# Reciprocals of the gate's real part on VectorE in place of exponentials on ScalarE

## The chip, the cores and the metric

The kernel runs on one core of one Trainium2 chip. The metric is the device time of one execution in microseconds (us). Before the change the median of three runs is 189.34 us (189.3 to 189.58). Four compute engines work side by side, each with its own instruction stream: TensorE (PE in the profile, PEld for its weight loads), VectorE (DVE), ScalarE (ACT) and GpSimd (POOL). SyncE (SP) issues most of the loads and stores. An engine works through its own stream in order and waits at an instruction until what that instruction needs is done.

## The reference

A gated linear attention with complex gates is followed by a normalised two-layer network with a residual. Per batch and head there is a running complex state of 48 x 48 that decays and turns by the gate at every one of 768 time steps:

```python
mag = np.sqrt(a_re * a_re + a_im * a_im)
scale = np.minimum(mag, 0.999) / (mag + 1e-06)
a_re_n, a_im_n = (a_re * scale, a_im * scale)
for t in range(S):
    new_re = ar * S_re - ai * S_im
    new_im = ar * S_im + ai * S_re
    S_re, S_im = (new_re + kv, new_im)        # kv: outer product of k and v at t
    y[:, :, t] = np.einsum('bhd,bhde->bhe', q[:, :, t], S_re)
```

Then, on x, the heads of y side by side (4 x 768 x 384): `x + relu(norm(x) @ w_ch1) @ w_ch2`, with 384 and 1536 columns. All tensors are float32; a_re lies between 0.85 and 0.95.

## The kernel before, in words

**Tiling.** The 768 steps of each of the 4 batches are cut into 6 chunks of 128 steps, and two chunks make a pair. There are 12 pairs, P = 0 to 11, three to a batch. One pair's gates are a tile of 128 partitions by 768 elements (8 heads x 2 steps x 48 columns). Pair 0 is worked in two halves of 4 heads, so its gate operations have 384 elements and come twice (names 0.0 and 0.1); those of pair 1 have 768 (name 1.0).

**From gate to decay and angle.** With a_re and a_im loaded into the tiles `are` and `aim`, the steps of one pair (or half) X are, in order of need:

- ln.X (line 452, ScalarE): w = ln(are)
- iv.X (line 454, ScalarE): are = exp(-w), that is 1/are, written over the tile that ln.X has read
- r.X: r = aim * are, the ratio of imaginary to real part (VectorE or GpSimd, helper line 293)
- r2.X (line 462 where ScalarE does it, else helper line 293): r2 = r * r
- u.X (line 466, ScalarE): r2 = ln(1 + r2)
- l.X and lc.X (lines 470 and 473, VectorE): l = w + r2 / 2, the log of the gate's magnitude, and its cap
- dec.X (line 481, TensorE): sums of l over time; en.X and e.X (line 485, ScalarE) are exponentials of it
- th.X (line 489, ScalarE) is the arctangent of r, ph.X (lines 506 to 514, TensorE) its sums over time, and sine and cosine follow from those

From them come the scaled keys and queries (ke, qe, ks, qs), the products over a chunk (am, atm), the state (G), the output y and x, and then the two-layer network (mm1, relu, mm2, ot, st).

**What sets the order.** One table, PLAN, written out by hand, holds every step with the letter of the engine that does it: A is ScalarE, V VectorE, G GpSimd, S SyncE, P TensorE with its bank. The table's order is the order in each engine's stream. A name behind @ makes a GpSimd step wait for a VectorE step. Waits on data follow from what each step reads and writes.

**Buffers.** `are` has three tiles, used in turn: the load are.3.0 refills the tile of pair 0, and has to wait until r.0.0 and r.0.1 have read it. `w` has two. SyncE issues its loads in order, so a load that waits holds back those behind it.

**TensorE at the start.** The steps named warm (line 805) are matrix products whose results nobody reads; 32 of them stand ahead of dec.0.0 and 22 between dec.0.0 and dec.0.1.

u_th (line 327, VectorE) is a constant that the first ph needs.

Of the kernel before, what the change touches and what calls it, by code (L numbers as in the profile page):

```python
# [13 lines left out]
AF = mybir.ActivationFunctionType  # L14
# [22 lines left out]


PLAN = """
aim.0.0:A are.0.0:S pickf:V tab.log.0:A ln.0.0:A iv.0.0:A are.1.0:S gln:S ue:G cmean:G uth:V r.0.0:V are.0.1:S one:G  # L40
r2.0.0:A u.0.0:A l.0.0:V ln.1.0:A aim.0.1:S ln.0.1:A q.0.1:S iv.0.1:A pick:G@r.0.0 lc.0.0:V warm.0:P0 warm.1:P0
warm.2:P0 warm.3:P0 warm.4:P0 warm.5:P0 warm.6:P0 warm.7:P0 warm.8:P0 warm.9:P0 warm.10:P0 warm.11:P0 warm.12:P0
warm.13:P0 warm.14:P0 warm.15:P0 warm.16:P0 warm.17:P0 warm.18:P0 warm.19:P0 warm.20:P0 warm.21:P0 warm.22:P0
warm.23:P0 warm.24:P0 warm.25:P0 warm.26:P0 warm.27:P0 warm.28:P0 warm.29:P0 warm.30:P0 warm.31:P0 dec.0.0:P6
aim.1.0:S iv.1.0:A r.0.1:V r.1.0:V ident:G pad.e.0:G@r.0.1 are.2.0:S pad.e.1:G zdec:G@r.0.1 r2.1.0:V r2.0.1:A u.0.1:A
l.0.1:V u.1.0:A lc.0.1:V ln.2.0:A l.1.0:V lc.1.0:V q.0.0:S warm.32:P0 warm.33:P0 warm.34:P0 warm.35:P0 warm.36:P0
warm.37:P0 warm.38:P0 warm.39:P0 warm.40:P0 warm.41:P0 warm.42:P0 warm.43:P0 warm.44:P0 warm.45:P0 warm.46:P0
warm.47:P0 warm.48:P0 warm.49:P0 warm.50:P0 warm.51:P0 warm.52:P0 warm.53:P0 dec.0.1:P2 aim.2.0:S en.0.0:A6 pad.qs.2:G
# [103 lines left out]
class Graph:  # L152
# [5 lines left out]
    def add(self, name, emit, needs=(), uses=(), ps=None):  # L158
        assert name not in self.ops, name
        self.ops[name] = Op(name, emit, list(needs), list(uses), ps)  # L160
# [51 lines left out]
def kernel(  # L212
# [12 lines left out]
    nc = tc.nc  # L225
    B, H, S, D = q.shape
# [40 lines left out]
    def T(name, i):  # L267
        return tiles[name][i % RINGS[name]]

    g = Graph(RINGS)  # L270
    act = nc.scalar.activation

    def eng(name):
        return g.ops[name].eng

    def bank(owner, parts=C):
        return banks[0:parts, g.bank[owner]]

    def bank2(owner, parts=C):
        i = g.bank[owner]  # L280
        return banks[0:parts, i:i + 2]
# [16 lines left out]
    def flat(t):  # L298
        return t.rearrange("p h d -> p (h d)")


    ident = pool.tile([C, C], BF16, name="ident")
    u_th = pool.tile([C, R, R, C], FP16, name="u_th")
    u_e = pool.tile([C, R, R, C], FP16, name="u_e")
    pick = pool.tile([C, C], FP16, name="pick")
# [4 lines left out]
    cmean = pool.tile([C, C], FP32, name="cmean")  # L310
    gc = pool.tile([C, ND, C], BF16, name="gc")
    gln = pool.tile([C, ND], FP32, name="gln")
# [54 lines left out]
    for i in range(NG):  # L367
        g.add(f"wl.{i}", lambda i=i: nc.gpsimd.dma_start(
            out=w1b[:, :, ts(i, 512)], in_=moe_w_ch1.rearrange("(dc p) j -> p dc j", p=C)[:, :, ts(i, 512)]))
        g.add(f"wl.{NG + i}", lambda i=i: nc.gpsimd.dma_start(  # L370
            out=w2b[:, ts(i, JG)], in_=moe_w_ch2.rearrange("(jc p) e -> p jc e", p=C)[:, ts(i, JG)]))
# [11 lines left out]
    for jb in range(NG):  # L383
# [7 lines left out]
        for ec in range(ND):  # L391
            g.add(f"wc.{jb}.{ec}", lambda jb=jb, ec=ec, o=o: nc.vector.scalar_tensor_tensor(
                out=w1b[:, ec, ts(jb, 512)], in0=w1b[:, ec, ts(jb, 512)], scalar=gln[:, ds(ec, 1)],
# [3 lines left out]
    def pair_ops(P):  # L397
# [6 lines left out]
        add = g.add  # L404

        for c in range(R):
            for nm, ap in (("k", k), ("q", q), ("vf", v)):
                add(f"{nm}.{P}.{c}", lambda nm=nm, ap=ap, c=c: ring(f"{nm}.{P}.{c}").dma_start(  # L408
                    out=T(nm, P)[:, c],
                    in_=ap[b].rearrange("h (c p) d -> p c h d", p=C)[:, pp * R + c]),  # L410
# [13 lines left out]
        for i in range(NS):  # L424
            hs = ts(i, HS)
            fs = ts(i, W)
            X = f"{P}.{i}"

            def S_(name, n=P, hs=hs):
                return flat(T(name, n)[:, hs])  # L430

            def view(owner):
                if NS == 1:
                    return bank2(owner)[:, :, 0:W]
                return bank(owner)[:, 0:R * W].rearrange("p (c x) -> p c x", c=R)

            def v16(owner=f"ph.{X}", view=view):
                if NS == 1:
                    return bank2(owner).bitcast(I16).rearrange(
                        "p s (x two) -> p s x two", two=2)[:, :, 0:W, 0]  # L440
                return bank(owner).bitcast(I16)[:, 0:2 * R * W].rearrange(
                    "p (c x two) -> p c x two", c=R, two=2)[:, :, :, 0]
# [5 lines left out]
            for nm, ap in (("are", a_re), ("aim", a_im)):  # L448
                add(f"{nm}.{X}", lambda nm=nm, ap=ap, hs=hs, X=X: ring(f"{nm}.{X}").dma_start(
                    out=T(nm, P)[:, hs], in_=ap[b][hs].rearrange(  # L450
                        "h (k p j) d -> p k h (j d)", p=C, j=R)[:, pp]), uses=[(nm, P)])
            add(f"ln.{X}", lambda S_=S_: act(out=S_("w"), in_=S_("are"), func=AF.Ln),
                needs=[f"are.{X}"], uses=[("are", P), ("w", P)])
            add(f"iv.{X}", lambda S_=S_: act(out=S_("are"), in_=S_("w"), func=AF.Exp, scale=-1.0),  # L454
                needs=[f"ln.{X}"], uses=[("are", P), ("w", P)])
            add(f"r.{X}", lambda S_=S_, X=X: tt(f"r.{X}", out=S_("r"), in0=S_("aim"), in1=S_("are"),
                                                op=ALU.mult),
# [11 lines left out]
            def f_l(S_=S_):  # L469
# [4 lines left out]
                out=S_("l"), in0=S_("l"), scalar1=LNCAP, scalar2=LNEPS, op0=ALU.min, op1=ALU.add),  # L474
# [9 lines left out]
            for nm, sc in (("en", -1.0), ("e", 1.0)):  # L484
                add(f"{nm}.{X}", lambda nm=nm, sc=sc, X=X, fs=fs, view=view: act(  # L485
                    out=T(nm, P)[:, 0:R, fs], in_=view(f"dec.{X}"), func=AF.Exp, scale=sc),
# [34 lines left out]
            if not last:  # L521
# [11 lines left out]
                out=T("trig", P)[:, 1, :, fs], in_=v16(), func=AF.Sin, scale=TWO_PI_SAFE / TURN),  # L533
                needs=[f"ph.{X}"], uses=[("trig", P)], ps=(f"ph.{X}", nb))
            if P in QUARTER:
                def f_qt(X=X, view=view):
# [7 lines left out]
                    out=T("trig", P)[:, 0, :, fs], in_=v16(), func=AF.Sin, scale=TWO_PI_SAFE / TURN),  # L544
                    needs=[f"qt.{X}"], uses=[("trig", P)], ps=(f"ph.{X}", nb))
            else:
                def f_abs(X=X, fs=fs, v16=v16):
# [8 lines left out]
                    out=T("trig", P)[:, 0, :, fs], in_=T("sh", P)[:, :, fs], func=AF.Sin,  # L556
                    scale=-TWO_PI_SAFE / TURN, bias=PI / 2),
# [47 lines left out]
        for c in range(R):  # L605
# [26 lines left out]
            def f_am(n):  # L632
# [7 lines left out]
                out=T("atm", n), in_=bank2(f"am.{n}").rearrange("p s (h t) -> p (s h) t", t=C)),  # L640
# [122 lines left out]
        for c in range(R):  # L763
            n = P * R + c
            cuts = [(f".{x}", ts(x, DM // 2)) for x in range(2)] if n == NP * R - 1 else [("", ds(0, DM))]
            for tag, es in cuts:
                own = f"o.{n}{tag}"
                w = DM // len(cuts)
                for part in range(NG):
# [9 lines left out]
                    out=T("ot", n)[:, es], in_=bank(own)[:, 0:w], mul=T("rstd", P)[:, ds(c, 1)]),  # L779
# [3 lines left out]
                def f_ot(n=n, c=c, own=own, es=es, w=w, tag=tag):  # L783
# [12 lines left out]
                    out=out[b].rearrange("(c p) e -> p c e", p=C)[:, pp * R + c, es],  # L796
                    in_=T("ot", n)[:, es]),
                    needs=[f"ot.{n}{tag}"], uses=[("ot", n)])

    for P in range(NP):  # L800
        pair_ops(P)
# [40 lines left out]
```

## Time and profile before

| what | before |
|---|---|
| median of three runs | 189.34 us |
| span of the profiled execution | 187.1 us |
| TensorE busy | 176.4 us, 94% |
| ScalarE busy | 160.0 us, 86% |
| VectorE busy | 153.7 us, 82% |
| GpSimd busy | 111.1 us, 59% |
| iv on 384 elements (ScalarE, 2) | 523 ns each |
| iv on 768 elements (ScalarE, 11) | 844 ns each |

The span reaches from the first to the last instruction of the profiled execution; its full time isn't listed apart, and the runs' median is 2.24 us above the span. A row of the timeline reads: start in us from the span's start, length in us, engine, line, operation, what it writes and reads with shapes and types, how many instructions are merged, and in brackets how long the engine had been idle and what ended that. A tile shown as r may be r2, since the trace leaves numbers out. Tiles of before and after can be told apart by line.

### The profile page before, as it was taken

How to read it: one execution, taken by the hardware profiler on the slowest of the kernel's cores; microseconds unless marked ns; L12 is line 12 of the kernel's file. 1: busy time of each engine (PE TensorE's matmuls, PEld its weight loads, DVE VectorE, ACT ScalarE, POOL GpSimd, SP SyncE). 2: the span in 40 equal slices, each digit the busy share in tenths (PEclk: the TensorE clock that was granted, in tenths of full speed). 3: DMA queues.
4: the chain of work that ended last, by engine and by line, in shares of the span. 5: the costliest groups of instructions: out<-in, count | busy, mean ns of one | idle time of the engine just before them, and what ended most of it. 6: DMA issues, size and time to landing. Idle time of an engine off the chain costs nothing.

```text
span 187.1 us, 5110 instructions
## 1 busy us (share of the span) xinstructions
PE 176.4 (94%) x2025; PEld 135.1 (72%) x2027; DVE 153.7 (82%) x275; ACT 160.0 (86%) x228; POOL 111.1 (59%) x130
## 2 busy tenths in 40 slices
PE   5978898999999999999999999999999998999993
PEld 3756565787767789866687696878867866778772
DVE  1479999999989999999979989899879888866332
ACT  3889999999999989999999999998999897274560
POOL 3328699589207996288176692365879759420600
PEclk9999999999999999999999999999999999999999
DMA  5999999999999999699999997999999969996122
GB/s 148 291 256 227 223 260 189 207 206 194 233 261 239 219 221 191 128 203 309 204 155 238 256 265 92 185 247 169 216 175 215 203 144 229 210 199 173 40 90 84
DMA packets 132439, 37.39 MB, mean 200 GB/s; under 512 B 126528, under 2 KB 132416, under 8 KB 132416
## 3 DMA queue, kind: packets, MB, share of 16 engines
q1 hardware_dynamic: 123040, 32.45, 83.9%
q0 software_dynamic: 2784, 2.36, 8.2%
q10 hardware_dynamic: 6592, 2.26, 4.7%
q8 instruction: 16, 0.26, 0.6%
q14 instruction: 7, 0.06, 0.1%
HBM read 28.31 MB, written 4.72 MB: 177 GB/s over the span
## 4 chain that ended last, share of the span: by engine, by line
PE 71%; DVE 10%; DMA 6%; ACT 4%; POOL 3%; SPq 2%; issue 2%; DVEq 0%; POOLq 0%
PE banks L772 25%; PE banks L740 21%; PE banks L635 5%; PE banks L612 4%; PE banks L506 4%; PE banks L481 4%; DMA aim<-in_a_im_dram 3%; PE banks L685 2%; DMA qsT<-qs 2%; PE banks L706 2%; PE banks L688 2%; DMA are<-in_a_re_dram 2%; PE banks L663 2%; SPq L408 1%; DVE r L293 1%
## 5 line engine op out<-in xcount | busy, mean ns | idle before, releaser
L772 PE MATMUL banks<-w2b,h 128*128 128x384 bf16 (+1 forms) x300 | 53.8, 319 | 0.0
L740 PE MATMUL banks<-xT,w1b 128*128 128x256 bf16 x432 | 51.4, 272 | 0.2 <-DVE xT L290 0.2
L740 PEld LDWEIGHTS <-w1b 128*128 128x128 bf16 x432 | 41.3, 98 | 6.3 <-issue 0.4
L772 PEld LDWEIGHTS <-h 128*128 128x128 bf16 x300 | 27.1, 97 | 13.3
L293 DVE TENSOR_TENSOR atm<-banks,mask 128x1024 bf16<-128x1024 f32 x24 | 28.8, 1219 | 5.1 <-PE banks L635 5.0
L757 ACT ACTIVATE h<-banks 128x1024 bf16<-128x1024 f32 (+1 forms) x24 | 23.8, 1003 | 5.3 <-PE banks L740 5.1
L293 POOL TENSOR_TENSOR qe<-q,e 128x384 bf16<-128x384 f32 x19 | 17.5, 929 | 15.7 <-ACT e L485 9.1
L810 ACT ACT_TABLE_LOAD x19 | 24.4, 1283 | 1.7 <-PEq L826 1.3
L293 POOL TENSOR_TENSOR ke<-k,en 128x384 bf16<-128x384 f32 x16 | 14.8, 939 | 7.5 <-DVE qs L293 6.8
L759 DVE TENSOR_SCALAR h<-banks 128x1024 bf16<-128x1024 f32 (+1 forms) x13 | 15.2, 1169 | 3.6 <-PE banks L740 3.6
L805 PE MATMUL banks<-u_e 128*128 128x256 f16 x111 | 15.5, 297 | 2.2 <-POOL u_e L322 2.2
L635 PE MATMUL banks<-qsT,ksT 128*128 128x128 bf16 x192 | 14.1, 219 | 1.0 <-DMA qsT<-qs 0.7
L805 PEld LDWEIGHTS <-u_e 128*128 128x128 f16 x111 | 11.5, 106 | 4.5 <-POOL u_e L322 1.9
L293 POOL TENSOR_TENSOR r<-aim,are 128x768 f16<-128x768 f32 x7 | 12.6, 1811 | 3.0 <-ACT are L454 3.0
L635 PEld LDWEIGHTS <-ksT 128*128 128x128 bf16 x192 | 11.9, 98 | 2.5 <-issue 1.1
L293 POOL TENSOR_TENSOR qs<-qe,trig 128x768 bf16<-128x768 bf16 (+1 forms) x8 | 12.6, 1576 | 1.6 <-DVE qe L293 0.9
L470 DVE SCALAR_TENSOR_TENSOR l<-r,w 128x768 f16<-128x768 f16 (+1 forms) x13 | 12.3, 949 | 1.3 <-ACT r L466 1.1
L785 POOL TENSOR_TENSOR ot<-ot,x 128x384 f32<-128x384 f32 x11 | 10.5, 966 | 4.6 <-ACT ot L778 4.3
L698 DVE BATCH_NORM_STATS2 stats<-x 128x6 f32<-128x384 bf16 x24 | 13.1, 548 | 0.0
L288 ACT CAST x<-banks 128x384 bf16<-128x384 f32 x19 | 8.8, 478 | 5.0 <-PE banks L688 4.5
L293 POOL TENSOR_TENSOR ks<-ke,trig 128x768 bf16<-128x768 bf16 (+1 forms) x7 | 10.7, 1539 | 2.8 <-DVE qs L293 1.6
L685 PE MATMUL banks<-v,atm 128*128 128x48 bf16 x192 | 11.9, 183 | 0.0
(101 smaller groups left out, 380.4 us busy)
## 6 DMA issues: line engine op xcount, KB each, us to landing
q<-in_q_dram SPq DMA_DIRECT2D x24, 192.0 KB, 4.7
k<-in_k_dram SPq DMA_DIRECT2D x24, 192.0 KB, 4.5
are<-in_a_re_dram SPq DMA_DIRECT2D x11, 384.0 KB, 4.8
aim<-in_a_im_dram SPq DMA_DIRECT2D x11, 384.0 KB, 4.8
vf<-in_v_dram SPq DMA_DIRECT2D x19, 192.0 KB, 4.3
out_dram<-ot SPq DMA_DIRECT2D x18, 192.0 KB, 3.5
w1b<-in_moe_w_ch_dram POOLq DMA_DIRECT2D x3, 384.0 KB, 6.4
w2b<-in_moe_w_ch_dram POOLq DMA_DIRECT2D x3, 384.0 KB, 7.8
```

What stands on the lines that cost most here:

```text
L293: {"DVE": nc.vector, "POOL": nc.gpsimd}[eng(name)].tensor_tensor(**kw)
L470: nc.vector.scalar_tensor_tensor(out=S_("l"), in0=S_("r2"), scalar=0.5, in1=S_("w"), op0=ALU.mult, op1=ALU.add)
L635: nc.tensor.matmul(ps[:, h], lhsT=T("ksT", n)[:, h], rhs=T("qsT", n)[:, h], start=True, stop=True)
L685: nc.tensor.matmul(ps[:, h], lhsT=T("atm", n)[:, h], rhs=T("v", P)[:, c, h], start=True, stop=nfirst)
L698: nc.vector.bn_stats(out=T("stats", n), in_=T("x", n))
L740: nc.tensor.matmul(ps[:, jj], lhsT=w1b[:, dc, ts(gi * JG + jj, C)], rhs=T("xT", P)[:, dc].rearrange("p c t -> p (c t)"), start=(dc == 0), ...
L757: act(out=dst, in_=src, func=AF.Relu)
L759: nc.vector.tensor_scalar(out=dst, in0=src, scalar1=0.0, scalar2=None, op0=ALU.max)
L772: nc.tensor.matmul(bank(own)[:, 0:w], lhsT=T("h", P)[:, j, ts(c, C)], rhs=w2b[:, j, es], start=(j == 0), stop=(j == NJ - 1))
L785: nc.gpsimd.tensor_tensor(out=T("ot", n)[:, es], in0=T("ot", n)[:, es], in1=T("x", n)[:, es], op=ALU.add)
L805: g.add(f"warm.{i}", lambda i=i: nc.tensor.matmul(bank(f"warm.{i}")[:, 0:256], lhsT=u_e[:, 0, 0], rhs=u_e[:, 1].rearrange("p j t -> p (j t ...
L810: g.add(f"tab.{nm}.{i}", lambda tab=tab: nc.scalar.preload_act_table_set(tab))
```

## The change

The iv steps of pair 0 (both halves) and of pair 1 go from ScalarE to VectorE, where they are a reciprocal of `are` itself, written in place. The logarithms ln.0.0, ln.0.1 and ln.1.0 stay, since l needs w. The iv steps of the other ten pairs stay as they were. In PLAN three letters change, and no step changes its place:

```diff
-aim.0.0:A are.0.0:S pickf:V tab.log.0:A ln.0.0:A iv.0.0:A are.1.0:S gln:S ue:G cmean:G uth:V r.0.0:V are.0.1:S one:G
-r2.0.0:A u.0.0:A l.0.0:V ln.1.0:A aim.0.1:S ln.0.1:A q.0.1:S iv.0.1:A pick:G@r.0.0 lc.0.0:V warm.0:P0 warm.1:P0
+aim.0.0:A are.0.0:S pickf:V tab.log.0:A ln.0.0:A iv.0.0:V are.1.0:S gln:S ue:G cmean:G uth:V r.0.0:V are.0.1:S one:G
+r2.0.0:A u.0.0:A l.0.0:V ln.1.0:A aim.0.1:S ln.0.1:A q.0.1:S iv.0.1:V pick:G@r.0.0 lc.0.0:V warm.0:P0 warm.1:P0
...
-aim.1.0:S iv.1.0:A r.0.1:V r.1.0:V ident:G pad.e.0:G@r.0.1 are.2.0:S pad.e.1:G zdec:G@r.0.1 r2.1.0:V r2.0.1:A u.0.1:A
+aim.1.0:S iv.1.0:V r.0.1:V r.1.0:V ident:G pad.e.0:G@r.0.1 are.2.0:S pad.e.1:G zdec:G@r.0.1 r2.1.0:V r2.0.1:A u.0.1:A
...
-            add(f"iv.{X}", lambda S_=S_: act(out=S_("are"), in_=S_("w"), func=AF.Exp, scale=-1.0),
+            def f_iv(S_=S_, X=X):
+                if eng(f"iv.{X}") == "DVE":
+                    nc.vector.reciprocal(out=S_("are"), in_=S_("are"))
+                else:
+                    act(out=S_("are"), in_=S_("w"), func=AF.Exp, scale=-1.0)
+            add(f"iv.{X}", f_iv,
                 needs=[f"ln.{X}"], uses=[("are", P), ("w", P)])
```

VectorE's stream at the start, before the change: u_th, then r.0.0, l.0.0 and lc.0.0, then r.0.1, r.1.0 and r2.1.0 (84 and 85 are the r tiles of pairs 0 and 1, 64 and 65 their are tiles, 88 is r2 of pair 1; in brackets the semaphores that a row waits for, Activation_49 being ScalarE's):

```order
L327 TENSOR_SCALAR u_th<-u_e 128x512 [waits Pool_49]
L293 TENSOR_TENSOR r_84<-aim_67,are_64 128x384 [waits DMAHW1_49,DMAHW0_49,Activation_49]
L470 SCALAR_TENSOR_TENSOR l_89<-r_87,w_82 128x384 [waits Activation_49]
L473 TENSOR_SCALAR l_89<-l_89 128x384 [waits DVE_49]
L293 TENSOR_TENSOR r_84<-aim_67,are_64 128x384 [waits DMAHW5_49,DMAHW4_49,Activation_49]
L293 TENSOR_TENSOR r_85<-aim_68,are_65 128x768 [waits DMAHW7_49,DMAHW2_49,Activation_49]
L293 TENSOR_TENSOR r_88<-r_85 128x768 [waits DVE_49]
```

The same place in VectorE's stream after the change (lines below 451 are the same, later ones five higher):

```order
L456 RECIPROCAL are_64<-are_64 128x384 [waits DMAHW1_49,Activation_49]
L327 TENSOR_SCALAR u_th<-u_e 128x512 [waits Pool_49]
L293 TENSOR_TENSOR r_84<-aim_67,are_64 128x384 [waits DMAHW0_49,DVE_49]
L475 SCALAR_TENSOR_TENSOR l_89<-r_87,w_82 128x384 [waits Activation_49]
L456 RECIPROCAL are_64<-are_64 128x384 [waits DMAHW4_49,Activation_49]
L478 TENSOR_SCALAR l_89<-l_89 128x384 [waits DVE_49]
L456 RECIPROCAL are_65<-are_65 128x768 [waits DMAHW2_49]
L293 TENSOR_TENSOR r_84<-aim_67,are_64 128x384 [waits DMAHW5_49,DVE_49]
L293 TENSOR_TENSOR r_85<-aim_68,are_65 128x768 [waits DMAHW7_49,DVE_49]
L293 TENSOR_TENSOR r_88<-r_85 128x768 [waits DVE_49]
```

Three reciprocals have come in: one ahead of u_th, one between l.0.0 and lc.0.0, one ahead of r.0.1. The first two wait for ScalarE, whose logarithm reads the tile that they overwrite; the third's logarithm stands ahead of the second's, so it needs no wait of its own.

ScalarE's stream at the start, before the change: ln.0.0, iv.0.0, r2.0.0, u.0.0, ln.1.0, ln.0.1, iv.0.1, iv.1.0, r2.0.1, u.0.1, u.1.0:

```order
L452 ACTIVATE w_82<-are_64 128x384 [waits DMAHW1_49]
L454 ACTIVATE are_64<-w_82 128x384 [waits Activation_49]
L462 ACTIVATE r_87<-r_84 128x384 [waits DVE_49]
L466 ACTIVATE r_87<-r_87 128x384 [waits Activation_49]
L452 ACTIVATE w_83<-are_65 128x768 [waits DMAHW2_49]
L452 ACTIVATE w_82<-are_64 128x384 [waits DMAHW4_49]
L454 ACTIVATE are_64<-w_82 128x384 [waits Activation_49]
L454 ACTIVATE are_65<-w_83 128x768
L462 ACTIVATE r_87<-r_84 128x384 [waits DVE_49]
L466 ACTIVATE r_87<-r_87 128x384 [waits Activation_49]
L466 ACTIVATE r_88<-r_88 128x768 [waits DVE_49]
```

And after the change:

```order
L452 ACTIVATE w_82<-are_64 128x384 [waits DMAHW1_49]
L467 ACTIVATE r_87<-r_84 128x384 [waits DVE_49]
L471 ACTIVATE r_87<-r_87 128x384 [waits Activation_49]
L452 ACTIVATE w_83<-are_65 128x768 [waits DMAHW2_49]
L452 ACTIVATE w_82<-are_64 128x384 [waits DMAHW4_49]
L467 ACTIVATE r_87<-r_84 128x384 [waits DVE_49]
L471 ACTIVATE r_87<-r_87 128x384 [waits Activation_49]
L471 ACTIVATE r_88<-r_88 128x768 [waits DVE_49]
```

The three rows of line 454 are gone, and the other rows stand in the same order.

## The prediction

> **What bounds the kernel now.** I read the page's first part, then the busy time by stretches, and then the first twelve microseconds row by row.
>
> ```profile
> span 187.1 us, 5110 instructions
> PE 176.4 (94%) x2025; PEld 135.1 (72%) x2027; DVE 153.7 (82%) x275; ACT 160.0 (86%) x228; POOL 111.1 (59%) x130
> core 0: us, PE busy (x) PEld busy (x) DVE busy (x) ACT busy (x) POOL busy (x), PEclk, DMA share, GB/s
> 12.00:15.00 3.00, 2.76 (x25) 2.14 (x24) 2.09 (x3) 2.94 (x6) 1.49 (x2) 1.00 1.12 244
> 18.00:21.00 3.00, 2.36 (x31) 1.95 (x29) 2.87 (x7) 2.92 (x7) 1.96 (x5) 1.00 1.21 196
> 33.00:36.00 3.00, 2.63 (x58) 2.45 (x54) 2.90 (x7) 3.00 (x6) 1.37 (x1) 1.00 0.97 187
> 80.00:100.00 20.00, 20.00 (x212) 14.28 (x210) 17.58 (x32) 19.80 (x29) 12.08 (x14) 1.00 1.10 222
> ```
>
> The reader is to see two regimes. From 12 us on ScalarE hardly stops (2.94, 2.92 and 3.00 of 3 us), and later TensorE is full (20.00 of 20). Neither has room to catch up, so work that enters this stream late ends late. What decides when the stream begins is the chain ahead of it. These are ScalarE's rows (start, length, operation), and then VectorE's:
>
> ```profile
> 4.14 0.52 ACT L452 ACTIVATE w<-are 128x384 f32<-128x384 f32 x1 [1.52 <-DMA are<-in_a_re_dram]
> 4.70 0.52 ACT L454 ACTIVATE are<-w 128x384 f32<-128x384 f32 x1
> 5.84 0.52 ACT L462 ACTIVATE r<-r 128x384 f16<-128x384 f16 x1 [0.62 <-DVE r L293]
> 6.40 0.52 ACT L466 ACTIVATE r<-r 128x384 f16<-128x384 f16 x1
> 6.83 1.24 ACT L452 ACTIVATE w<-are 128x768 f32<-128x768 f32 x2
> 8.10 1.26 ACT L454 ACTIVATE are<-w 128x384 f32<-128x384 f32 x2
> 9.26 0.51 ACT L462 ACTIVATE r<-r 128x384 f16<-128x384 f16 x1
> 9.80 0.52 ACT L466 ACTIVATE r<-r 128x384 f16<-128x384 f16 x1
> 10.97 0.84 ACT L466 ACTIVATE r<-r 128x768 f16<-128x768 f16 x1 [0.65 <-DVE r L293]
> ```
>
> ```profile
> 2.20 0.29 DVE L327 TENSOR_SCALAR u_th<-u_e 128x512 f16<-128x512 f16 x1 [0.96 <-POOL u_e L322]
> 5.25 0.56 DVE L293 TENSOR_TENSOR r<-aim,are 128x384 f16<-128x384 f32 x1 [2.76 <-ACT are L454]
> 6.95 0.56 DVE L470 SCALAR_TENSOR_TENSOR l<-r,w 128x384 f16<-128x384 f16 x1 [1.14 <-ACT r L466]
> 7.55 0.26 DVE L473 TENSOR_SCALAR l<-l 128x384 f16<-128x384 f16 x1
> 8.65 0.56 DVE L293 TENSOR_TENSOR r<-aim,are 128x384 f16<-128x384 f32 x1 [0.85 <-ACT are L454]
> 9.39 0.96 DVE L293 TENSOR_TENSOR r<-aim,are 128x768 f16<-128x768 f32 x1 [0.17 <-ACT are L454]
> 10.38 0.56 DVE L293 TENSOR_TENSOR r<-r 128x768 f16<-128x768 f16 x1
> 10.86 0.55 DVE L470 SCALAR_TENSOR_TENSOR l<-r,w 128x384 f16<-128x384 f16 x1
> ```
>
> The row at 10.97 (u.1.0, line 466) is my mark: ScalarE waits 0.65 us for r2.1.0 on VectorE, and behind it the full stream starts. I therefore work out when u.1.0 starts after the change, and take its delay for the kernel's.
>
> **The change, removed.** Three exponentials leave ScalarE: 0.52 us at 4.70 and 1.26 us for the pair at 8.10, 1.78 us in all. ScalarE waits in this stretch anyway, so this pays only where it lets VectorE go sooner. It does not: each reciprocal overwrites the tile that its logarithm reads, so it still waits for that logarithm, and stands where the exponential stood (4.70 and about 8.1 us). The trig and log tables and their loads stay as they are.
>
> **Added: three reciprocals on VectorE, one after another.** No row of before shows one. The nearest rows are these, first VectorE's multiplies by shape and its one-source pass over float32, then two operations of GpSimd on one tiny tile, an add (L725) and a power (L727):
>
> ```profile
> L293 DVE TENSOR_TENSOR r<-aim,are 128x768 f16<-128x768 f32 x4 | 3.8, 955 | 1.0 <-ACT are L454 1.0
> L293 DVE TENSOR_TENSOR r<-aim,are 128x384 f16<-128x384 f32 x2 | 1.1, 558 | 3.6 <-ACT are L454 3.6
> L418 DVE TENSOR_SCALAR v<-vf 128x768 bf16<-128x768 f32 x3 | 1.6, 549 | 0.0
> L725 POOL TENSOR_SCALAR rstd<-mv 128x2 f32<-128x2 f32 x7 | 2.5, 351 | 12.3 <-DVE mv L699 10.2 <-DVE l L473 2.0
> L727 POOL TENSOR_TENSOR rstd<-rstd,half_n 128x2 f32<-128x2 f32 x7 | 5.0, 710 | 0.6
> ```
>
> A multiply costs 955 - 558 = 397 ns for 384 more elements, 1.03 ns each, over a fixed 558 - 397 = 161 ns. Call 1.03 ns a step. At s steps an element, a reciprocal takes R1 = 0.161 + 0.397 s for 384 elements and R2 = 0.161 + 0.794 s for 768. The cheap end is the v row: 0.549 for 768 and, at half the slope, 0.549 - 0.199 = 0.35 for 384. The dear end is an estimate: a float32 quotient has 24 bits, each found from the remainder of those before, so one bit a step would make s = 24. That a function can cost several times a simple operation is seen on GpSimd, where the power takes 710 ns against 351 for the add. Of the even cuts of 24 bits (24, 12, 8, 6, 4 or 3 steps) the mean in ratio is 7.4; **I take the nearest, 8**: R1 = 3.34, R2 = 6.51 us. This is an estimate, and the weakest number here.
>
> [...]
>
> **The sum**, with the gaps of the rows: a dependent operation starts 0.03 us after the one before it (10.38 behind 9.39 + 0.96), an independent one 0.08 before that ends (10.86 behind 10.38 + 0.56). The first reciprocal runs 4.70 to 4.70 + R1. u_th (0.29), done at 2.49 before, now stands behind it and ends 0.21 later, so r.0.0 starts at S = 4.70 + R1 + 0.13. From r.0.0 to the end of both logarithms the rows give 8.07 - 5.25 = 2.82, so the second reciprocal starts at S + 2.85. Behind it: lc.0.0 (0.26, 0.18 net), the third reciprocal (R2 less 0.08 overlap), r.0.1 (starts 0.08 early, ends at S + 3.43 + R1 + R2), r.1.0 (0.96 - 0.08), r2.1.0 (0.03 + 0.56), 0.03: u.1.0 starts at S + 4.93 + R1 + R2 = 9.76 + 2 R1 + R2. Against 10.97 the delay is 2 R1 + R2 - 1.21 = 1.588 s - 0.73: at s = 8 it is **+11.97 us**; each step more or less is 1.59.
>
> **Queued behind, and costed at nothing beside this.** On GpSimd the making of pick waits for r.0.0, the pads of e for r.0.1 and the w1b loads for lc.1.0; all have the delayed stream as cover, since what uses them is delayed as much. The loads stand on one row:
>
> ```profile
> 11.48 1.02 SPq L449 DMA_DIRECT2D are<-in_a_re_dram  x1
> ```
>
> This load, are.3.0, refills the tile that r.0.1 reads. r.0.1 now ends at 8.26 + 2 R1 + R2 = 21.45, so the load and every one behind it on SyncE start 10 us late. That is 2 us less than the compute, so loads are not the last wait. Were they, the delay would be 10.0; so the sum's lower side at eight steps is 199.3. TensorE's rows:
>
> ```profile
> 2.22 5.60 PE L805 MATMUL banks<-u_e 128*128 128x256 f16 x32 [2.22 <-POOL u_e L322]
> ...
> 8.19 2.56 PE L805 MATMUL banks<-u_e 128*128 128x256 f16 x22
> 11.75 0.49 PE L481 MATMUL banks<-l,u_e 128*128 128x192 f16 x4 [1.00 <-DVE l L473]
> 12.08 0.93 PE L805 MATMUL banks<-u_e 128*128 128x256 f16 x7
> 13.25 0.81 PE L481 MATMUL banks<-l,u_e 128*128 128x384 f16 x4 [0.24 <-DVE l L473]
> ```
>
> The first fillers took 5.60 / 32 = 0.175 us each, the later ones 2.56 / 22 = 0.116, at a granted clock of 1.00 by the stretches shown. At eight steps TensorE is left idle from 7.8 to lc.0.0 at 14.5. If it is slow again, the stretch from dec.0.1 to the end of dec.1.0 (11.75 to 14.06, of which 0.24 is a wait, so 2.07 of work) grows by half, 1.04, of which the wait covers 0.24: e.1.0 on ScalarE comes some 0.8 us later, and at a doubled pace 1.8. No row of before shows TensorE after such a pause, so I leave this out of the sum and keep it in the range. [...]
>
> The profiled span is 187.1, and the median of the runs, 189.34, lies 2.24 above it; I take that margin as unchanged: 187.1 + 11.97 + 2.24 = **201.3 us**.
>
> **Rivals.**
> - *One step per element.* R1 = 0.56, R2 = 0.96: the delay is +0.87 (0.13 from u_th, the rest from three VectorE operations and lc.0.0 in series where ScalarE and VectorE overlapped before); 190.2 us. For it: every elementwise row of VectorE runs at a step or less. Against it: each of them is a copy, multiply, add or compare. Chance 0.20.
> - *The reciprocal at the fast pass of the v row* (not slower). 2 R1 + R2 = 1.25, which meets the break-even of 1.21: 189.4 us; below it, by less than 0.3 us, the kernel is faster. For it: one source, float32, as in v. Against it: v is a scale and shift. Chance 0.04.
> - *Two to five steps*: 191.8 to 196.6 us, 0.05. *More than nine*: from 204.5 us at ten up to 226.7 at the dear end, 24; 0.05; the range leaves this case out.
> - *The change does not do what it says*: were the reciprocal free of the logarithm it could run during it and save 0.56 us once; the wait on ScalarE in its row speaks against this, and it is in no case above.
>
> **How the numbers follow.** Forecast (six to nine steps): 0.66, 198.1 to 202.9 us, to 203.7 with slow matmuls. One step 0.20, fast 0.04, two to five 0.05, more than nine 0.05. The range needs the one-step case: 189.9 to 204.0. A measurement of this kernel tells some 0.2% (0.4 us) from no change. A quarter of the one-step case could be absorbed (0.05), with the fast case 0.09 in all: faster 0.03, same 0.06, slower 0.91.
>
> **What would show it.** The rows of the three reciprocals: about 3.3, 3.3 and 6.5 us; u.1.0 starting near 23 us; VectorE nearly full from 11 to 24 us and ScalarE idle some 12 us more in all before 24; the load at 11.48 moved to about 21.5; the stretches behind alike, only later. Reciprocals of 0.6 and 1.0 us make the first rival right. A wrong step would be: rows as forecast but a time under 199, which would mean that the stream from 12 us on had room after all.

## The result, and the profile after

| | before | after |
|---|---|---|
| median of four runs | 189.46 us (189.3 to 190.81) | 197.61 us (197.48 to 199.38) |
| ratio, 95% interval | | 1.0411 (1.0342 to 1.048) |
| span of the profiled execution | 187.1 us | 195.7 us |
| profiled execution | | 197.66 us |

The kernel is 8.15 us slower by the medians and 8.6 us by the two spans. The page of after, its first and second part (busy times; then the clock granted to TensorE in tenths, by fortieths of the span):

```profile
span 195.7 us, 5111 instructions
PE 178.8 (91%) x2025; PEld 136.6 (70%) x2027; DVE 162.5 (83%) x278; ACT 158.1 (81%) x225; POOL 111.0 (57%) x130
...
PEclk9978699999999999999999999999999999999999
```

VectorE has 8.8 us more work (153.7 before) and ScalarE 1.9 less (160.0 before); what the change adds is more than four times what it removes. TensorE's clock, steady before, dips in the third to fifth slice. These are VectorE's rows at the start (start and length in us, line, operation):

```profile
4.54 2.55 DVE L456 RECIPROCAL are<-are 128x384 f32<-128x384 f32 x1 [3.30 <-ACT w L452]
7.01 0.23 DVE L327 TENSOR_SCALAR u_th<-u_e 128x512 f16<-128x512 f16 x1
7.15 0.55 DVE L293 TENSOR_TENSOR r<-aim,are 128x384 f16<-128x384 f32 x1
8.84 0.56 DVE L475 SCALAR_TENSOR_TENSOR l<-r,w 128x384 f16<-128x384 f16 x1 [1.14 <-ACT r L471]
9.99 2.55 DVE L456 RECIPROCAL are<-are 128x384 f32<-128x384 f32 x1 [0.59 <-ACT w L452]
12.46 0.20 DVE L478 TENSOR_SCALAR l<-l 128x384 f16<-128x384 f16 x1
12.57 4.94 DVE L456 RECIPROCAL are<-are 128x768 f32<-128x768 f32 x1
17.43 1.36 DVE L293 TENSOR_TENSOR r<-aim,are 128x384 f16<-128x384 f32 x2
18.82 0.56 DVE L293 TENSOR_TENSOR r<-r 128x768 f16<-128x768 f16 x1
```

The three reciprocals stand in series. The first two wait for ScalarE's logarithm (`ACT w L452`), the third follows at once, and r2.1.0 comes at 18.82 instead of 10.38. ScalarE's rows show the other side, idle 8.00 us for r.0.1, then u.1.0 at 19.41, and a second wait, for TensorE, ahead of e.1.0 at 23.43:

```profile
8.72 1.24 ACT L452 ACTIVATE w<-are 128x768 f32<-128x768 f32 x2
17.95 0.52 ACT L467 ACTIVATE r<-r 128x384 f16<-128x384 f16 x1 [8.00 <-DVE r L293]
18.51 0.52 ACT L471 ACTIVATE r<-r 128x384 f16<-128x384 f16 x1
19.41 0.84 ACT L471 ACTIVATE r<-r 128x768 f16<-128x768 f16 x1 [0.38 <-DVE r L293]
...
23.43 0.81 ACT L490 ACTIVATE e<-banks 128x768 bf16<-128x768 f32 x1 [0.96 <-PE banks L486]
```

Now e.1.0 is 4.02 us behind u.1.0. Before the change it was 3.13 us behind it, with no wait:

```profile
14.10 0.81 ACT L485 ACTIVATE e<-banks 128x768 bf16<-128x768 f32 x1
```

TensorE's rows tell why (L486 is dec, L810 the fillers), and so do the stretches, whose granted clock stands third from the end of each row:

```profile
12.71 0.80 PE L486 MATMUL banks<-l,u_e 128*128 128x192 f16 x4 [5.10 <-DVE l L478]
13.30 3.91 PE L810 MATMUL banks<-u_e 128*128 128x256 f16 x22
20.19 0.80 PE L486 MATMUL banks<-l,u_e 128*128 128x192 f16 x4 [2.98 <-DVE l L478]
20.79 1.70 PE L810 MATMUL banks<-u_e 128*128 128x256 f16 x7
22.28 1.12 PE L486 MATMUL banks<-l,u_e 128*128 128x384 f16 x4
```

```profile
core 0: us, PE busy (x) PEld busy (x) DVE busy (x) ACT busy (x) POOL busy (x), PEclk, DMA share, GB/s
12.70:16.00 3.30, 3.29 (x17) 2.45 (x17) 3.30 (x1) 0.00 (x0) 0.00 (x0) 0.50 0.21 36
20.20:22.20 2.00, 2.00 (x11) 1.59 (x11) 1.32 (x2) 2.00 (x5) 0.25 (x1) 0.50 1.24 276
24.00:36.00 12.00, 10.40 (x102) 7.41 (x101) 10.23 (x25) 11.60 (x20) 8.89 (x16) 1.00 1.08 204
```

TensorE pauses 5.10 and 2.98 us, and behind each pause it is granted half its clock (0.50). Seven fillers take 1.70 us (0.93 before), and dec.0.1 to dec.1.0 last from 20.19 to 23.40, where before it was 11.75 to 14.06. From 24 us on the stream is as before, only later, up to one late product (below): the first mm1 starts at 46.05 instead of 36.73, 9.32 us later, just as e.1.0 is (9.33).

### The profile page after: what moved, and what is told of

Read it like the earlier page. It is cut to its first block, busy times and chain, and to the rows that moved or that the text cites. A ratio compares the mean times of both kernels' runs of the same rounds, so it can differ in the third digit from the quotient of the medians.

```text
span 195.7 us, 5111 instructions
## 1 busy us (share of the span) xinstructions
PE 178.8 (91%) x2025; PEld 136.6 (70%) x2027; DVE 162.5 (83%) x278; ACT 158.1 (81%) x225; POOL 111.0 (57%) x130
## 4 chain that ended last, share of the span: by engine, by line
PE 73%; ACT 9%; DVE 7%; issue 7%; DMA 2%; ACTq 0%; DVEq 0%
PE banks L777 24%; PE banks L745 22%; PE banks L511 5%; PE banks L640 4%; PE banks L486 4%; PE banks L617 4%; PE banks L690 2%; ACT L815 2%; PE banks L711 2%; PE banks L693 2%; PE banks L668 2%; DMA are<-in_a_re_dram 2%; ACT w L452 1%; DVE r L293 1%; ACT e L490 1%
## 5 line engine op out<-in xcount | busy, mean ns | idle before, releaser
L810 PE MATMUL banks<-u_e 128*128 128x256 f16 x111 | 17.4, 320 | 2.2 <-POOL u_e L322 2.2
L486 PE MATMUL banks<-l,u_e 128*128 128x384 f16 (+1 forms) x52 | 10.8, 337 | 8.1 <-DVE l L478 8.1
L810 PEld LDWEIGHTS <-u_e 128*128 128x128 f16 x111 | 12.4, 114 | 5.4 <-POOL u_e L322 1.9
L293 POOL TENSOR_TENSOR r<-aim,are 128x768 f16<-128x768 f32 x7 | 12.6, 1813 | 3.0 <-ACT are L458 3.0
L293 POOL TENSOR_TENSOR qs<-qe,trig 128x768 bf16<-128x768 bf16 (+1 forms) x8 | 12.6, 1576 | 1.6 <-DVE qe L293 0.9
L475 DVE SCALAR_TENSOR_TENSOR l<-r,w 128x768 f16<-128x768 f16 (+1 forms) x13 | 12.3, 949 | 1.3 <-ACT r L471 1.1
L456 DVE RECIPROCAL are<-are 128x384 f32<-128x384 f32 (+1 forms) x3 | 10.0, 3349 | 3.9 <-ACT w L452 3.9
L486 PEld LDWEIGHTS <-u_e 128*128 128x128 f16 x52 | 5.3, 105 | 11.1 <-issue 9.0
```

The costliest lines, as they stand in the source:

```text
L293: {"DVE": nc.vector, "POOL": nc.gpsimd}[eng(name)].tensor_tensor(**kw)
L456: nc.vector.reciprocal(out=S_("are"), in_=S_("are"))
L475: nc.vector.scalar_tensor_tensor(out=S_("l"), in0=S_("r2"), scalar=0.5, in1=S_("w"), op0=ALU.mult, op1=ALU.add)
L486: nc.tensor.matmul(heads(ps[:, c]), lhsT=u_e[:, c, j], rhs=step(T("l", P), j), start=(j == 0), stop=(j == R - 1))
L810: g.add(f"warm.{i}", lambda i=i: nc.tensor.matmul(bank(f"warm.{i}")[:, 0:256], lhsT=u_e[:, 0, 0], rhs=u_e[:, 1].rearrange("p j t -> p (j t ...
```

## The experiments

**Theory.** The delay arises before 24 us: three reciprocals in series on VectorE ahead of u.1.0, and on top of them TensorE's half clock between u.1.0 and e.1.0. **Rivals:** the loads, since are.3.0 now waits for r.0.1; the move between engines as such, whatever the operation costs; the wait for the logarithm.

The marks of each profile follow. ln.0.0 starts when the first load has landed, which varies by 0.31 us; what the change does is in the third column. "Late wait" is TensorE's idle time at the products am of pairs 8 and later, read as a wait for a transposed tile that comes by DMA.

| run | ln.0.0 | u.1.0 - ln.0.0 | e.1.0 - u.1.0 | e.1.0 | span | span - e.1.0 | late wait |
|---|---|---|---|---|---|---|---|
| before | 4.14 | 6.83 | 3.13 | 14.10 | 187.1 | 173.0 | 0.7 |
| after | 3.98 | 15.43 | 4.02 | 23.43 | 195.7 | 172.3 | 0 |
| e1_pair0 | 3.93 | 10.64 | 4.91 | 19.48 | 191.7 | 172.2 | 0 |
| e2_pair1 | 3.98 | 10.42 | 4.39 | 18.79 | 191.0 | 172.2 | 0 |
| e3_multiply | 3.83 | 7.64 | 3.13 | 14.60 | 186.8 | 172.2 | 0 |
| e4_scale | 3.94 | 6.84 | 3.12 | 13.90 | 188.5 | 174.6 | 0.8 |
| e5_warm | 3.99 | 15.43 | 3.12 | 22.54 | 195.8 | 173.3 | 0.9 |
| e6_ring4 | 3.93 | 15.43 | 4.00 | 23.36 | 195.5 | 172.1 | 0 |
| e7_own_tile | 3.92 | 14.19 | 4.39 | 22.50 | 196.7 | 174.2 | 0.7 + 0.9 |
| e9_cold | 3.97 | 6.83 | 4.39 | 15.19 | 188.3 | 173.1 | 0.8 |
| e12_after | 3.99 | 15.43 | 4.39 | 23.81 | 196.0 | 172.2 | 0 |
| e5b_warm | 3.91 | 15.42 | 3.13 | 22.46 | 195.5 | 173.0 | 0.8 |
| e10_both | 4.04 | 14.19 | 3.13 | 21.36 | 194.9 | 173.5 | 1.0 |
| e11_half | 3.87 | 14.19 | 3.76 | 21.82 | 194.2 | 172.4 | 0 |

**One part of the change alone: e1_pair0, e2_pair1.**

```diff
# e1_pair0, from after (of PLAN's long lines only the steps concerned)
-aim.1.0:S iv.1.0:V r.0.1:V r.1.0:V
+aim.1.0:S iv.1.0:A r.0.1:V r.1.0:V
# e2_pair1, from after
-ln.0.0:A iv.0.0:V are.1.0:S
+ln.0.0:A iv.0.0:A are.1.0:S
...
-q.0.1:S iv.0.1:V pick:G@r.0.0
+q.0.1:S iv.0.1:A pick:G@r.0.0
```

> iv.1.0 is back on ScalarE; only pair 0's two reciprocals (2.55 us each) stay on VectorE. Chain theory (the three reciprocals stand in series ahead of u.1.0, and a slow TensorE adds to that): u.1.0 starts near 14.6 us instead of 10.97 (before) and 19.41 (changed), since the 4.94 us reciprocal is gone; TensorE still pauses 5 us, so the 22 fillers at half clock hold dec.0.1 until about 17.2 and e.1.0 starts near 19.1 us, 5.0 us later than before; time 193.8 to 194.5. Load rival (the time follows the load are.3.0, which waits for r.0.1): r.0.1 ends near 13.1, so the load starts 1.6 us later than before and the time is near 191.0.

> Only iv.1.0 (768 elements) is a reciprocal on VectorE; pair 0's two exponentials are back on ScalarE. Chain theory: the reciprocal runs from 7.7 to 12.7, r.0.1, r.1.0 and r2.1.0 follow, u.1.0 starts near 14.6 (3.7 us later than before); TensorE pauses about 4.7 us ahead of dec.0.1, and its half clock adds 0.9, so e.1.0 starts near 18.7; time 193.3 to 194.0. Load rival: r.0.1 ends near 13.1, the load moves by 1.6 us, time near 191.0.

Measured: 194.43 us (ratio 1.0228, 1.0171 to 1.0286) and 193.73 us (1.0194, 1.0132 to 1.0256), over a median of 190.26 for before on that chip. u.1.0 starts at 14.57 and 14.40, against 14.6 expected of both, and e.1.0 at 19.48 (19.1 expected) and 18.79 (18.7). The load rival's 191 us was reckoned from 189.34; from this chip's 190.26 it is 191.9, and both times still lie 1.8 us or more above it. VectorE's rows of e2_pair1, where the 768-element reciprocal stands alone:

```profile
7.38 0.26 DVE L478 TENSOR_SCALAR l<-l 128x384 f16<-128x384 f16 x1
7.56 4.95 DVE L456 RECIPROCAL are<-are 128x768 f32<-128x768 f32 x1
12.42 1.36 DVE L293 TENSOR_TENSOR r<-aim,are 128x384 f16<-128x384 f32 x2
```

r.0.1, whose own operands are there early, starts at 12.42 only because it is queued behind the other pair's reciprocal. In e1_pair0 the slow fillers (22 in 4.45 us, before 2.56) hold dec.0.1 to 17.53 (17.2 expected), and e.1.0 comes 4.91 us behind u.1.0, the most of all runs.

**Another operation in the reciprocals' place: e3_multiply, e4_scale.**

```diff
-                    nc.vector.reciprocal(out=S_("are"), in_=S_("are"))
# e3_multiply
+                    nc.vector.tensor_tensor(out=S_("are"), in0=S_("are"), in1=S_("are"), op=ALU.mult)
# e4_scale
+                    nc.vector.tensor_scalar(out=S_("are"), in0=S_("are"), scalar1=-1.25, scalar2=2.25,
+                                            op0=ALU.mult, op1=ALU.add)
```

> In the three places of the reciprocals VectorE multiplies the tile by itself instead (the kernel then computes with the gate's real part squared in place of its reciprocal): one step per element, same order, same waits. Chain theory: 0.56, 0.56 and 0.96 us, u.1.0 0.87 us later than before (11.8), time 189.7 to 190.3. Rival (moving the work between engines costs in itself, by the waits across engines): over 191.

> In the three places of the reciprocals VectorE does a scale and shift (a straight line near 1/a for a from 0.85 to 0.95, not the reciprocal): the fast one-source pass over float32. Chain theory: 0.35, 0.35 and 0.55 us, which is 1.25 against the break-even of 1.21: u.1.0 at 11.0, time 189.2 to 189.7, no change. Rival (ScalarE's 1.78 us less of work pays by itself): 188.9 or less.

Measured: 189.69 us (ratio 0.9976, 0.9946 to 1.0006) and 189.56 us (0.9967, 0.9935 to 0.9998). The groups of line 456 by shape, first of after, then of e3_multiply, then of e4_scale (count, busy us, mean ns of one):

```profile
L456 DVE RECIPROCAL are<-are 128x384 f32<-128x384 f32 x2 | 5.1, 2553 | 3.9 <-ACT w L452 3.9
L456 DVE RECIPROCAL are<-are 128x768 f32<-128x768 f32 x1 | 4.9, 4940 | 0.0
```

```profile
L456 DVE TENSOR_TENSOR are<-are 128x384 f32<-128x384 f32 x2 | 1.1, 558 | 3.7 <-ACT w L452 3.7
L456 DVE TENSOR_TENSOR are<-are 128x768 f32<-128x768 f32 x1 | 0.9, 950 | 0.0
```

```profile
L456 DVE TENSOR_SCALAR are<-are 128x384 f32<-128x384 f32 x2 | 0.7, 361 | 3.8 <-ACT w L452 3.8
L456 DVE TENSOR_SCALAR are<-are 128x768 f32<-128x768 f32 x1 | 0.6, 554 | 0.0
```

Order, engines and waits are those of the change; only the price differs. By 2 R1 + R2 - 1.21 u.1.0 should be late by 0.86 (multiply), 0.07 (scale) and 8.84 us (reciprocal); the third column gives 0.81, 0.01 and 8.60. So at the front the move itself costs nothing that the three durations don't explain, and the rival that it does is out (e3_multiply would have been over 191). The times alone say less. e3_multiply was forecast 0.4 to 1.0 us slower than before and came out 0.5 faster, although it is 0.8 us later at the front; this is taken up below. e4_scale came out 0.6 us faster than before, which is also what the rival "ScalarE's 1.78 us pay by themselves" forecast; what speaks against that rival is the front, where u.1.0 moved by 0.01 us. Neither kernel computes the reciprocal any more.

**TensorE's clock: e5_warm, e9_cold.** In e5_warm (run again as e5b_warm) fillers fill both pauses; in e9_cold the kernel before loses the 54 fillers ahead of dec.0.1, which leaves the clock's price without any reciprocal.

```diff
# e5_warm, from after: 43 and 36 more fillers (name.. stands for a row of them)
-warm.31:P0 dec.0.0:P6
+warm.31:P0 warm.111..153:P0 dec.0.0:P6
...
-warm.53:P0 dec.0.1:P2
+warm.53:P0 warm.154..189:P0 dec.0.1:P2
# e9_cold, from before: warm.0 to warm.53 left out of PLAN
```

> The changed kernel with 43 more fillers ahead of dec.0.0 and 36 more ahead of dec.0.1, so that TensorE has work in both of its pauses. Clock theory (the pauses halve TensorE's clock, and dec.0.1 to dec.1.0 at half clock delay e.1.0 by 0.9 us beyond u.1.0): granted clock 1.00 throughout, u.1.0 unchanged at 19.4, e.1.0 near 22.5 instead of 23.43, time about 196.7. Rival (the clock is hidden behind ScalarE): e.1.0 and the time unchanged, 197.6.

> The kernel before, with the first 54 fillers left out: TensorE has nothing to do until dec.0.0 and between it and dec.0.1, and no reciprocal is on VectorE. Clock theory: granted clock near 0.5 at dec.0.1 and dec.1.0, u.1.0 unchanged at 11.0, e.1.0 near 15.0 instead of 14.10, time 189.6 to 190.3. Rival (the clock costs nothing there): no change, 189.4.

Measured: e5_warm 197.74 us (ratio 1.0415, 1.0351 to 1.0478), e9_cold 190.51 (1.0048, 1.0012 to 1.0085). At the front e.1.0 came where the clock theory has it: it stands 3.12 us behind u.1.0 with fillers, as before the change, and 4.39 behind it in e9_cold. TensorE in e9_cold (L476 is dec):

```profile
11.58 0.80 PE L476 MATMUL banks<-l,u_e 128*128 128x192 f16 x4 [3.10 <-DVE l L468]
12.17 1.70 PE L800 MATMUL banks<-u_e 128*128 128x256 f16 x7
13.67 1.49 PE L476 MATMUL banks<-l,u_e 128*128 128x384 f16 x4
```

The same seven fillers take 1.70 us and dec.1.0 1.49 instead of 0.81, with no reciprocal in the kernel: the slow TensorE costs 0.9 us in after and 1.3 in e9_cold. One part of the expectation failed: the granted clock on record reads 1.00 all through e9_cold, where 0.5 was expected. So a recorded 1.00 at a kernel's start did not mean full pace here; the length of the rows shows it. But the 196.7 us expected of e5_warm did not come. Its front is 0.89 us earlier and stays so (first mm1 at 45.16 instead of 46.05) until one late row, of which this is TensorE's in e5_warm:

```profile
167.72 0.61 PE L640 MATMUL banks<-qsT,ksT 128*128 128x128 bf16 x8 [0.91 <-ACT ot L783]
```

and this, of the two kernels' same product, before and after the change:

```profile
159.01 0.61 PE L635 MATMUL banks<-qsT,ksT 128*128 128x128 bf16 x8 [0.71 <-DMA qsT<-qs]
```

```profile
167.44 0.61 PE L640 MATMUL banks<-qsT,ksT 128*128 128x128 bf16 x8
```

Before the change TensorE waits 0.71 us there for a transposed query tile, after it not at all, and with the fillers 0.91. The row of e5_warm names ot on ScalarE instead (as those of e5b_warm, e9_cold and e4_scale do). But the changed kernel starts the same product at 167.44, before that ot (167.79), so the product doesn't need it. The tile's transfer, issued at 163.61 and landing 3.9 us later, fits the wait. In this profile, then, the gain is given back where the tile hasn't come, and in the same way the change's 9.33 us at e.1.0 become 8.6 at the end of its profiled span. Between the medians a gain of 0.9 us could not be told apart from none: the ratio's interval is wider than that.

**The loads, and the wait for the logarithm: e6_ring4, e7_own_tile.**

```diff
# e6_ring4, from after
-RINGS = {"are": 3, "aim": 3,
+RINGS = {"are": 4, "aim": 3,
# e7_own_tile, from after (rec(P) is a float32 view of a tile h, unused until 39 us; r reads it)
-                    nc.vector.reciprocal(out=S_("are"), in_=S_("are"))
+                    nc.vector.reciprocal(out=flat(rec(P)[:, hs]), in_=S_("are"))
```

> The changed kernel with four tiles for the gate's real part instead of three, so that the load are.3.0 need not wait for r.0.1. Chain theory (the compute is the last wait): the load goes back from 17.95 to about 11 us, u.1.0 and e.1.0 stay at 19.4 and 23.4, time 197.6 within 0.4. Load rival (the stalled loads carry part of the delay): the time falls by 1 us or more.

> The changed kernel with the reciprocals written to a place of their own (the relu output's tiles, not in use before 39 us), so that they wait for the load alone and not for the logarithm. Chain theory: the first starts as the load lands (4.0 instead of 4.54), the second right behind l.0.0 (about 8.2 instead of 9.99), so u.1.0 starts near 18.2 instead of 19.41 and the time is near 196.4; still 7 us over before, since the three reciprocals' 10 us of VectorE remain in series. Rival (the wait for the logarithm is what costs): a much larger gain, under 193.

Measured: 197.52 us (ratio 1.0406, 1.0337 to 1.0475) and 197.35 us (1.041, 1.0339 to 1.048). The load are.3.0 on SyncE, after the change and in e6_ring4:

```profile
17.95 0.37 SPq L449 DMA_DIRECT2D are<-in_a_re_dram  x1
```

```profile
11.30 1.13 SPq L449 DMA_DIRECT2D are<-in_a_re_dram  x1
```

It starts 6.65 us sooner, and u.1.0 and e.1.0 don't move (0.07 us or less, as the first load landed 0.05 sooner), nor does the span beyond 0.2 us: the load rival is out at the front and in the profiled execution; the medians alone resolve about a microsecond (the next load of that kind still waits, until 17.89, so the queue isn't wholly freed). In e7_own_tile the second reciprocal starts right behind l.0.0:

```profile
8.22 0.56 DVE L480 SCALAR_TENSOR_TENSOR l<-r,w 128x384 f16<-128x384 f16 x1 [1.14 <-ACT r L476]
8.70 2.55 DVE L460 RECIPROCAL h<-are 128x384 f32<-128x384 f32 x1
```

u.1.0 comes 1.24 us sooner behind the first logarithm, as expected. But e.1.0 follows it by 4.39 us instead of 4.02, and two late waits (0.74 and 0.89) take the rest. The 0.37 us are not the edit's doing, since the unaltered change shows the same 4.39 in e12_after below. The time missed the 196.4 expected; its six executions lie from 196.61 to 198.79, and the profiled one, at 198.68, is not typical of them. That the wait for the logarithm is the cost, which would have given under 193, is out.

**Together, and the price by bytes: e12_after, e5b_warm, e10_both, e11_half**, on one chip. e12_after is the change unaltered, e10_both is e7_own_tile with e5_warm's fillers, and e11_half writes e7_own_tile's reciprocals as 16-bit floats:

```diff
# e11_half, from e7_own_tile (the line around the call and its indent are left out here)
-        return tiles["h"][P].rearrange("p j t -> p (j t)").bitcast(FP32)[:, 0:H * R * D].rearrange(
+        return tiles["h"][P].rearrange("p j t -> p (j t)").bitcast(FP16)[:, 0:H * R * D].rearrange(
```

> The changed kernel once more, unaltered, beside the two that follow, so that they are compared with it on one chip. Expected: e.1.0 at 23.4 us again and a time of 197.5 to 198 us; how far its runs lie apart shows what the loads' landing does to the rest of the kernel.

> The version with 79 more fillers once more. In its first profile e.1.0 started at 22.54 instead of 23.43, so the 0.89 us were won back at the front, but TensorE then stood 0.9 us at one late product (waiting for a transposed query tile that comes by DMA), and the time stayed at 197.7. Theory that the late wait is chance: it is gone in some of these runs, and the median is 0.5 us or more below the unaltered kernel's. Theory that the loads set a second limit close behind the compute: the time is the unaltered kernel's again, within 0.3 us.

> Both at once: reciprocals in a place of their own, so that they do not wait for the logarithms, and 79 more fillers. Chain theory: u.1.0 near 18.1, e.1.0 near 21.2, 2.2 us earlier than in the changed kernel; if nothing else limits, 195.4 us, and if the loads set a second limit within a microsecond, about 196.5. Still some 6 us over before, since 10 us of reciprocals stand in series on VectorE.

> Reciprocals in a place of their own and rounded to 16-bit floats as they are written. What it tells: whether the price of a reciprocal goes by the element (six steps each, 2.55 and 4.94 us as before) or by the bytes written (then about half of that). Expected: by the element, 2.55 and 4.94; r behind them may be faster by its smaller input.

Measured, with before at 190.19 us: 198.76 (196.74 to 199.68), 197.64 (197.5 to 199.54), 196.68 (196.4 to 197.12) and, of two runs, 196.48 us. e12_after missed its expectation: e.1.0 is at 23.81 instead of 23.4, and the median lies above 197.5 to 198.

```profile
23.81 0.81 ACT L490 ACTIVATE e<-banks 128x768 bf16<-128x768 f32 x1 [1.33 <-PE banks L486]
```

The same kernel as after, with u.1.0 at the same place, thus loses 1.26 us to TensorE's pace in place of 0.89. The difference lies in how long the half clock lasts. Cut into windows of 0.1 us, every stretch of half clock in the seven profiles that have one is about 3.4 us long or twice that. After the change it runs from 12.6 to 16.1 and from 19.4 to 22.9 us, in e12_after from 12.3 to 15.8 and from 19.1 to 26.0.

e5b_warm lies 1.1 us under e12_after, which is what the theory of chance forecast (0.5 or more) and not the other (within 0.3). But the unaltered change spreads over 2.9 us on this chip, and e5b_warm's profile has the late wait again (0.76), so neither is settled. e10_both has both gains at the front (e.1.0 at 21.36), waits 1.01 us at the late product and stays 6.5 us over before (ratio 1.0352, 1.03 to 1.0403). Its time fits the forecast with a second limit (196.5); against e12_after, though, it is 2.1 us faster, near the 2.2 forecast without one. e11_half's groups:

```profile
L461 DVE RECIPROCAL h<-are 128x384 f16<-128x384 f32 x2 | 5.1, 2549 | 2.6 <-DMA are<-in_a_re_dram 2.6
L461 DVE RECIPROCAL h<-are 128x768 f16<-128x768 f32 x1 | 4.9, 4940 | 0.0
```

The price goes by the element, not by the bytes written. No run that computes the reciprocal on VectorE comes near the kernel before.

**What stays open.** Span less e.1.0 falls into two groups: 172.1 to 172.4 us in the seven profiles without a late wait, 173.0 to 174.6 in the seven with one. In e4_scale more was lost, on GpSimd, where a query load came late:

```profile
23.00 0.92 POOL L293 TENSOR_TENSOR qe<-q,e 128x384 bf16<-128x384 f32 x1 [3.14 <-DMA q<-in_q_dram]
```

Which profiles have the late wait does not follow from e.1.0 alone (e3_multiply at 14.60 has none, e9_cold at 15.19 has 0.8), and no run set the landing of these transfers. That the loads form a second limit within a microsecond of the compute fits five of the six profiles in which e.1.0 follows u.1.0 by 3.13 us or less; it isn't shown.

## Why the prediction was right, and where it was off

- **What bounds.** Right: the stream behind 12 us had no room. The first mm1 is as late as e.1.0, to 0.01 us.
- **Removed: nothing gained at the front.** Right: the first two reciprocals waited for their logarithms (starts 4.54 and 9.99), the third needed no wait, and e4_scale shows no gain from ScalarE's 1.78 us.
- **Price of a reciprocal.** This is the mis-sized term. Eight steps an element were estimated, 3.34 and 6.51 us; measured are 2.553 and 4.940. The slope is (4940 - 2553) / 384 = 6.22 ns an element, 6.0 of the 1.03 ns steps, over a fixed 166 ns: the form R = 0.161 + step x s held, with s = 6. At the term's 1.59 us a step, two steps are 3.2 of the 3.7 us between the forecast 201.3 and the measured 197.61. That eight came as near as it did was partly luck: a quotient of 24 bits, cut evenly into steps, was the author's estimate, and no row bears it out.
- **The sum.** With the measured durations it gives 8.84 us at u.1.0 against 8.60 from the logarithm on. The remaining quarter of a microsecond lies in overlaps, such as u_th's 0.23 instead of 0.29 and 1.36 for r.0.1 and r.1.0 together, where 1.44 was reckoned. The other small terms come to another quarter: 0.89 us of slow TensorE came on top, 0.71 of a late wait and 0.16 of the first load's landing fell away, and so did 0.28 of the margin. A time lies 1.96 us above its own span in the profiled execution; the 2.24 of the sum set a median against another execution's span.
- **The range.** The time lies in the stated range (189.9 to 204.0), but 0.5 us under the band of six to nine steps that had most of the chance; the range went lower only to take in the one-step case. The sign of a wrong step, rows as forecast but a time under 199, did not occur: the time is under 199 because the rows were shorter.
- **TensorE's pace.** Left out of the sum at a price of 0.8 us, it came at 0.89 and, in the second profile of the same kernel, at 1.26. That the first fillers ran at a granted clock of 1.00 was read from stretches that begin at 12 us; it is on record so, but e9_cold has the same record where seven fillers take 1.70 us instead of 0.93. The 0.8 us would have been right to add: the granted clock is 0.50 behind both pauses of after, 5.10 and 2.98 us long. The length of the pause alone does not decide it here, though: in e11_half 0.50 came even after a pause of 1.99 us, and in e7_own_tile the stretch right behind a pause of 3.65 us ran at 1.00 (below).
- **The loads.** Right that they are not the last wait at the front (e6_ring4): are.3.0 starts 6.47 us later than before and u.1.0 8.44, the 2 us less that was forecast. Not foreseen was that the kernel before loses 0.71 us at a late transposed tile, which the profiled execution after does not, so the profiled end moves by 0.7 less than the front.
- **Rivals.** One step an element (190.2 us) fell by the rows themselves; e3_multiply shows that its arithmetic was right at the front (0.81 us against 0.87). The fast pass met its break-even in e4_scale: u.1.0 0.01 us later, where 0.04 was forecast.

## What to carry to other kernels

Before an operation moves to an emptier engine, price it there in steps per element: here a division took six steps on VectorE, where a multiply took one, so 1.8 us less on one engine became 10 us more on the other. An idle engine at the start of a kernel isn't free if the step lies on the chain that starts the saturated stream; count what stands in series, and what is queued behind it on that engine (r.0.1 waited for another pair's reciprocal). When an upstream delay leaves TensorE waiting, add the slow products behind the wait, as a range: here 0.9 to 1.3 us for one and the same kernel.

## What the runs showed of the hardware that was not expected

- A reciprocal on VectorE takes 6.22 ns an element whether it writes float32 or 16-bit floats (4.940 us for 768 elements both ways).
- The half clock follows a pause of TensorE, but not by the pause's length alone. It came behind pauses of 2.98 us (after) and 1.99 us (e11_half, second row below), and not right behind one of 3.65 us (e7_own_tile, first row, where TensorE starts again at 11.41). With fillers in the pauses the clock stayed at 1.00 (e5_warm, 7.6 to 23.4 us). Each stretch of it lasted about 3.4 or 6.8 us (from 12.6 to 16.1 in after, from 19.1 to 26.0 in e12_after), so one kernel's loss varied: e.1.0 came 4.02 us behind u.1.0 in after and 4.39 in e12_after. What sets where a stretch begins isn't shown.

```profile
11.40:14.30 2.90, 2.89 (x26) 2.48 (x26) 2.90 (x1) 0.00 (x0) 0.00 (x0) 1.00 0.95 196
20.30:21.70 1.40, 1.36 (x5) 0.67 (x5) 0.54 (x1) 0.82 (x2) 1.09 (x2) 0.50 1.17 229
```

- The kernel before, rerun beside the experiments, lay in most executions between 188.09 and 191.52 us, and the change between 196.74 and 199.68 on one chip. The front up to u.1.0 repeats to 0.01 us from the first logarithm on (15.42 and 15.43 in five profiles whose reciprocals are those of the change). What varied in the profiles lies behind u.1.0: how long TensorE's half clock lasts, and the late waits.
